# Three float32r passes of 12-bit parts in place of float32 matmuls with Strassen's form

## The chip, the cores and the metric

The kernel runs on one core of one Trainium2 chip. A core has TensorE (matmuls, whose results go to the memory PSUM), VectorE, ScalarE, GpSimd, and SyncE, which here only issues DMA transfers. The metric is the device time of one execution in microseconds, the median of several; the profile is one such execution. The kernel before took 689.4 us (three runs, 688.28 to 691.62).

## The reference

Two blocks follow each other: lightning attention over blocks of 64 tokens with a decaying state, and a two-layer block with a leaky ReLU.

```python
# q, k, v: (4, 8, 768, 64) float32; w_in (512, 2048), w_out (2048, 512) float64
for b in range(nb):                                   # blocks of 64 tokens
    intra = einsum('bhic,bhjc->bhij', qb, kb) * Dmask
    intra = einsum('bhij,bhjd->bhid', intra, vb)
    inter = einsum('bhid,bhde->bhie', qb * lam_pow, kv_state)
    out[:, :, sl] = intra + inter
    kv_state = lam_block * kv_state + einsum('bhsd,bhse->bhde', kb * rev_pow, vb)
x = out.transpose(0, 2, 1, 3).reshape(3072, 512)
h = x @ w_in                                          # "up"
return maximum(0.01 * h, h) @ w_out                   # "down", float32 (3072, 512)
```

The weights come as float64 and are made float32 on the chip, by integer operations on the two words of each number. The two large products, 3072 x 512 x 2048 each, are to have float32's precision, so one pass of a narrow type is not enough.

## The kernel before

It works on chunks of 128 tokens (24 of them) and groups of four chunks (six). Attention runs in float32 on TensorE: transposes of k and q, and 64x64 matmuls in the four quarters of the array ("quads").

```python
def quad(out, rows, lhsT, rhs, cols, start=False):
    nc.tensor.matmul(out[HALF[cols]], lhsT=lhsT[HALF[rows]], rhs=rhs[HALF[rows]], ...)
# a chunk: transpose k, transpose q (4 matmuls each), scores (16 quads), kv (16),
# own (16: scores times v), inter (16: state times q); then ONE copy into x:
run("ACT", 0.6, lambda: nc.scalar.copy(x, po.pop(b)[:, :, 0:HP, :]), ["inter"], ("x", b))
```

The large products are float32 matmuls in Strassen's form (Winograd's variant): seven half-size products in place of eight, with sums of quarters of x, of the weights and of the leaky ReLU's result g formed on VectorE and GpSimd. Up and down of a quarter of d_ff ("unit" u) follow each other, so g stays in SBUF. Two PSUM tags, Z and W, alternate.

```python
PROD = {"P1": ("A11", "B11"), "P2": ("A12", "B21"), "P3": ("S4", "B22"), "P4": ("A22", "T4"),
        "P5": ("S1", "T1"), "P6": ("S2", "T2"), "P7": ("S3", "T3")}
    ...
    def mult(tag, name, after, first=False):                  # one product, booked at us = 1.73
        if tag not in st:
            st[tag] = pp.tile([P, UP, T], F32, name=tag, tag=bank[tag])
        run("PE", us, lambda: mm(st[tag], name, first), after, tag)
    return [lambda: (mult("Z", "P1", ins("P1"), True), keep(0, "Z")),        # keep: copy by ScalarE
            lambda: (mult("W", "P2", ["tot1"] + ins("P2"), True), total(0, "W")),   # total: add by VectorE
            ...  # P6, P5, P7, P3, P4

# up: mm of one product                          (T = 256 columns, UP = 2)
for i in range(UP):
    for kk in range(2):
        nc.tensor.matmul(t[:, i, :], lhsT=w[:, kk, :], rhs=x[:, kk, :], ...)         # L571
# down: mm of one product                        (4 matmuls again)
        nc.tensor.matmul(t[:, m, :], lhsT=G[g, u][sa][:, i, m * P:(m + 1) * P],
                         rhs=WO[UP * u + i][:, SB[sb], :], ...)                      # L597
...
for n, (g, u, w) in enumerate((g, u, w) for g in range(NG) for u in range(NU) for w in range(2)):
    need((2 * u + w + 1) * NW // (2 * NU))                    # weights converted just ahead of use
    together((up, down)[w](g, u) if n else parts, ...)        # attention's parts in between
```

A half of a 256-wide pair of weights is loaded as float64 (512 KB) and made float32 by three ScalarE operations (the magnitude, and two that extract low bits) and VectorE operations (a shift and an integer add). A small scheduler in the kernel (`run`, with a duration booked for each step) decides the order in which instructions are issued; each engine then works in that order.

Of the kernel before, what the change touches and what calls it, by code (L numbers as in the profile page):

```python
# [8 lines left out]
F32 = mybir.dt.float32  # L37
I64 = mybir.dt.int64
I32 = mybir.dt.int32
# [6 lines left out]

def _bc(ap, idx, n):

    a = [list(x) for x in ap.ap]
    return bass.AP(ap.tensor, ap.offset, a[:idx] + [[0, n]] + a[idx:])  # L50


@with_exitstack
def kernel(
# [12 lines left out]
    B, H, S, D = q.shape  # L67
    C = P
    C2 = C // 2
    NCB = S // C  # L70
# [3 lines left out]
    FO = d_ff // P  # L74
# [3 lines left out]
    T = GC * C // 2  # L78
    NP = FO // 2
    HD = d_model // 2  # L80
    UP = 2
    NU = NP // UP
    NX = 3
    WARM = 10
    HALF = (slice(0, D), slice(D, 2 * D))
    assert D == 64 and KO == HP == 4 and S % C == 0 and NCH % GC == 0 and NP % UP == 0

    const = ctx.enter_context(tc.tile_pool(name="const", bufs=1))
    wop = ctx.enter_context(tc.tile_pool(name="wop", bufs=1))
    ldp = ctx.enter_context(tc.tile_pool(name="ldp", bufs=2))  # L90
    atp = ctx.enter_context(tc.tile_pool(name="atp", bufs=1))
    xp = ctx.enter_context(tc.tile_pool(name="xp", bufs=1))
    tp = ctx.enter_context(tc.tile_pool(name="tp", bufs=2))
    PS = bass.MemoryType.PSUM
    pp = ctx.enter_context(tc.tile_pool(name="pp", bufs=1, space=PS))

    ctx.enter_context(tc.manual_schedule(engines=None))


    lam_b = const.tile([P, H], F32, name="lam_b")  # L100
    nc.scalar.dma_start(out=lam_b, in_=lam.partition_broadcast(P))
    ident = const.tile([P, P], F32, name="ident")
    make_identity(nc, ident)

    idle = pp.tile([P, 2 * P], F32, name="idle", tag="W")
    for _ in range(WARM):
        nc.tensor.transpose(out=idle[:, 0:P], in_=ident, identity=ident)
    zero = const.tile([P, 1], F32, name="zero")
    nc.gpsimd.memset(zero, 0.0)

    lam_h = const.tile([P, H], F32, name="lam_h")
    lam_p = const.tile([P, HP], F32, name="lam_p")
    for i in range(2):
        nc.vector.tensor_copy(lam_h[:, i * HP:(i + 1) * HP], lam_b[:, i::2])
    for i in range(2):
        nc.vector.tensor_copy(lam_p[HALF[i]], lam_h[HALF[i], i::2])


    eye = atp.tile([P, C2], F32, name="eye", tag="sc")
    nc.vector.tensor_tensor(eye, ident[:, 0:C2], ident[:, C2:C], op=ALU.add)  # L120
    decay = const.tile([P, 2, HP, C2], F32, name="decay")
    for hi in range(2):
        for hp in range(HP):
            nc.vector.tensor_tensor_scan(decay[:, hi, hp, :], _bc(lam_h[:, 2 * hp + hi], 1, C2), eye, 0.0,
                                         op0=ALU.mult, op1=ALU.add)

    pow_q = const.tile([P, HP, C2], F32, name="pow_q")
    for hp in range(HP):
        nc.vector.tensor_tensor_scan(pow_q[:, hp, :], _bc(lam_p[:, hp], 1, C2), _bc(zero[:, 0], 1, C2), 1.0,
                                     op0=ALU.mult, op1=ALU.add)  # L130
    pow_k = decay[:, :, :, C2 - 1].rearrange("p hi hp -> p hp hi")
    lam_c = pow_q[:, :, C2 - 1]


    state = [const.tile([P, HP, D], F32, name=f"state{i}") for i in range(4)]

    QB = 2 * P
    SB = {"B21": 0, "B11": 1, "T4": 2, "B22": 3, "T1": 4, "T3": 5, "T2": 6, "B12": 2}  # L140
    WI, WO = [None] * NP, [None] * NP
    w_in_r = moe_w_in.rearrange("(ko ki) n -> ki ko n", ki=P)

    blocks = [(w, p, h) for u in range(NU) for w in ("wi", "wo") for p in range(UP * u, UP * u + UP) for h in range(2)]
    NW = len(blocks)

    ROOMS = ["st"] + [f"{w}{p}" for w, p, h in reversed(blocks) if h == 0 and p >= UP]


    LOADS = "cwcwcwwcwwwwwcwwcccwcwwcwwwwwwwwwwwwwwwwww" + "c" * NCH
    SLACK, AHEAD = (0.7, 0.3), (10.0, 14.0)

    T_DVE = [0, 4, 7, 9, 11, 15]

    FIRST, STEPS = 2, [2, 2, 1, 5, 5, 6, 3, 3, 0, 1, 0, 2, 0, 1, 0, 4]
    rooms = {}
    w_raw, lo, w_done = {}, {}, 0

    clk = {"PE": 0.0, "ACT": 2.0, "DVE": 8.0, "POOL": 1.0, "DMA": 0.5}

    ready, later = {}, {"ACT": [], "DVE": [], "DVE T": [], "POOL T": []}

    def run(eng, us, fn, after=(), gives=None, fill=True):
        t = max([ready.get(k, 0.0) for k in after], default=0.0)  # L170
        for e in (eng, eng + " T") if fill else ():
            while later.get(e) and emit(e, t + SLACK[alone]):
                pass
        clk[eng] = max(clk[eng], t) + us
        fn()
        if gives is not None:
            ready[gives] = clk[eng] + 0.1
        if eng != "DMA":
            pump()

    def emit(queue, until):

        can, us, fn, after, gives = later[queue][0]
        eng = queue.split()[0]
        if not can() or held and eng != queue or any(k not in ready for k in after):
            return False
# [50 lines left out]

# [458 lines left out]
```

## Time and profile before

| | |
|---|---|
| time | 689.4 us (688.28 to 691.62) |
| span of the profiled execution | 686.1 us |
| HBM read, written | 35.66 MB, 6.29 MB |
| a 128x512 float32 copy from PSUM on ScalarE | 585 to 592 ns |
| a 128x512 float32 sum with one PSUM operand on VectorE | 0.68 to 0.69 us |
| loads of 512 KB of weights, from issue to landing | 5.1 to 5.5 us |

In the profile, PE is the matmul side of TensorE and PEld its weight loads; DVE is VectorE, ACT ScalarE, POOL GpSimd, and SPq the queue of SyncE. A row of groups or of the timeline gives the source line, engine, operation, destination and sources by their names in the program, and the shape. The chain of waits is followed back from the last instruction, at each step to what released it. "PEclk" is the clock that TensorE was granted, in tenths of full speed, with 9 for 90% or more. The ends of matmuls are modelled, and their durations overlap, so the pace of matmuls is read from starts and not from durations.

### The profile page before, as it was taken

Reading aid. Unit: us, or ns where it says so; the run is one execution under the profiler, and the core shown is the slowest. Engines: PE = TensorE matmul, PEld = TensorE weight load, DVE = VectorE, ACT = ScalarE, POOL = GpSimd, SP = SyncE. Lnnn points to the kernel's source line nnn. Section 1 sums busy time; section 2 is a strip of 40 time slices with the busy share of each in tenths; the row PEclk is TensorE's granted clock in tenths of the full one; section 3 lists DMA queues with packets and bytes.
Section 4 is the critical chain, followed back from the end, with each engine's and each line's share of the span. In section 5 each row is a group of like instructions: output and inputs, shape, how many; then the busy total and the mean of one; then the engine's idle time right before and its main releaser. Section 6 shows DMA issues by size and latency. Waiting matters only on the chain.

```text
span 686.1 us, 13341 instructions
## 1 busy us (share of the span) xinstructions
PE 672.5 (98%) x5834; PEld 580.3 (85%) x5834; DVE 319.2 (47%) x474; ACT 213.2 (31%) x361; POOL 145.1 (21%) x141
## 2 busy tenths in 40 slices
PE   7799999999999999999999999999999999999997
PEld 6588888888888888888888888888888888888886
DVE  5897898572342552424425315244234245325324
ACT  5778866422222122230220321202122211221210
POOL 3565457551001033010113211204000003000000
PEclk9999999999999999999999999999999999999999
DMA  8996574513001004120210301000100000100001
GB/s 220 291 303 208 150 200 127 152 48 93 16 1 32 1 25 123 24 48 0 48 32 16 109 5 28 1 1 1 62 1 0 1 1 15 47 0 1 1 0 62
DMA packets 89050, 42.81 MB, mean 62 GB/s; under 512 B 76704, under 2 KB 82848, under 8 KB 88992
## 3 DMA queue, kind: packets, MB, share of 16 engines
q1 hardware_dynamic: 88848, 41.95, 22.0%
q8 instruction: 46, 0.75, 0.4%
q14 instruction: 12, 0.10, 0.0%
q10 hardware_dynamic: 144, 0.00, 0.0%
HBM read 35.66 MB, written 6.29 MB: 61 GB/s over the span
## 4 chain that ended last, share of the span: by engine, by line
PE 93%; DMA 3%; DVE 2%; SPq 1%; issue 1%; ACT 0%; POOL 0%; DVEq 0%
PE Z L571 24%; PE Z L597 23%; PE W L571 18%; PE W L597 18%; PE po L338 3%; PE pt L354 3%; DMA k<-in_k_dram 2%; PE ps L338 2%; PE pu L338 1%; DVE gS L542 1%; DVE gA L542 1%; DMA q<-in_q_dram 0%; SPq L327 0%; DVE os L521 0%; DVE wo L286 0%
## 5 line engine op out<-in xcount | busy, mean ns | idle before, releaser
L597 PE MATMUL Z<-wo,gA 128*128 128x256 f32 x576 | 137.5, 382 | 0.0
L597 PEld LDWEIGHTS Z<-wo,gA 128*128 128x128 f32 x576 | 107.8, 190 | 14.8
L571 PE MATMUL Z<-x,wi 128*128 128x256 f32 x384 | 92.2, 383 | 0.0
L571 PE MATMUL W<-xs,wi 128*128 128x256 f32 x384 | 92.0, 382 | 0.0
L597 PE MATMUL W<-wo,gA 128*128 128x256 f32 x384 | 91.0, 380 | 0.0
L571 PE MATMUL Z<-xs,wi 128*128 128x256 f32 x384 | 90.9, 380 | 0.0
L517 ACT COPY gA<-Z 128x512 f32<-128x512 f32 x48 | 28.1, 586 | 179.1 <-PE Z L571 178.8
L571 PEld LDWEIGHTS Z<-x,wi 128*128 128x128 f32 x384 | 72.7, 192 | 10.2 <-DVE wi L286 0.3
L571 PEld LDWEIGHTS Z<-xs,wi 128*128 128x128 f32 x384 | 72.8, 190 | 10.0
L597 PEld LDWEIGHTS W<-wo,gA 128*128 128x128 f32 x384 | 72.7, 190 | 10.0
L533 ACT ACTIVATE gA<-gA 128x512 f32<-128x512 f32 x72 | 45.3, 630 | 112.3 <-DVE gA L521 112.0
L571 PEld LDWEIGHTS W<-xs,wi 128*128 128x128 f32 x384 | 71.3, 190 | 9.6
L366 POOL TENSOR_TENSOR k<-k,decay 128x512 f32<-128x512 f32 (+1 forms) x24 | 27.6, 1150 | 219.7 <-PE pt L354 214.6
L521 DVE TENSOR_TENSOR gA<-gA,W 128x512 f32<-128x512 f32 x48 | 32.9, 686 | 87.3 <-PE W L571 87.3
L521 DVE TENSOR_TENSOR gA<-gA,Z 128x512 f32<-128x512 f32 x24 | 16.5, 687 | 97.8 <-PE Z L571 97.8
L420 POOL TENSOR_TENSOR state<-state,pow_q 128x256 f32<-128x256 f32 x40 | 28.1, 702 | 95.9 <-DVE state L417 89.2
L597 PE MATMUL W<-wo,gS 128*128 128x256 f32 x192 | 46.1, 383 | 0.5 <-DVE os L521 0.5
L597 PE MATMUL Z<-wo,gS 128*128 128x256 f32 x192 | 45.7, 381 | 0.5 <-DVE os L515 0.5
L571 PE MATMUL W<-x,wi 128*128 128x256 f32 x192 | 45.5, 380 | 0.0
L521 DVE TENSOR_TENSOR os<-os,W 128x512 f32<-128x512 f32 x48 | 32.8, 682 | 23.5 <-PE W L597 23.5
L597 PEld LDWEIGHTS W<-wo,gS 128*128 128x128 f32 x192 | 35.7, 189 | 6.9 <-DVE os L521 1.9
L597 PEld LDWEIGHTS Z<-wo,gS 128*128 128x128 f32 x192 | 36.0, 190 | 6.0 <-DVE os L515 0.9
(76 smaller groups left out, 721.9 us busy)
## 6 DMA issues: line engine op xcount, KB each, us to landing
ws<-in_moe_w_in_dram SPq DMA_DIRECT2D x16, 512.0 KB, 5.5
ws<-in_moe_w_out_dram SPq DMA_DIRECT2D x16, 512.0 KB, 5.1
k<-in_k_dram SPq DMA_DIRECT2D x48, 128.0 KB, 3.3
q<-in_q_dram SPq DMA_DIRECT2D x48, 128.0 KB, 2.9
v<-in_v_dram SPq DMA_DIRECT2D x24, 256.0 KB, 3.6
out_dram<-os SPq DMA_DIRECT2D x23, 256.0 KB, 2.1
out_dram<-os SPq DMA_DIRECT2D x2, 128.0 KB, 1.7
lam_b<-in_lam_dram ACTq DMA_DIRECT2D x1, 4.0 KB, 2.7
```

The source lines that it names most:

```text
L338: nc.tensor.matmul(out[HALF[cols]], lhsT=lhsT[HALF[rows]], rhs=rhs[HALF[rows]], start=start, stop=True, skip_group_check=True)
L354: nc.tensor.transpose(out=pt[:, y, :], in_=loaded[c][i][:, 2 * y:2 * y + 2, :].rearrange("p a d -> p (a d)"), identity=ident)
L366: run("POOL", 1.2, lambda: nc.gpsimd.tensor_tensor(kr[n], kr[n], _bc(pow_k, 3, D)[n], op=ALU.mult), [("pt", "k")], ("kd", c))
L420: run("POOL", 0.8, lambda: nc.gpsimd.tensor_tensor(state[(m + 1) % 4], new, _bc(lam_c, 2, D), op=ALU.mult), [("state", m)], ("lstate", m + 1))
L517: run("ACT", 0.6, lambda: nc.scalar.copy(dst(i), st[tag]), [tag], f"keep{i}")
L521: lambda: nc.vector.tensor_tensor(dst(i), dst(i), st[tag], op=ALU.add), [f"keep{i}", tag], f"tot{i}")
L533: run("ACT", 0.64, lambda: nc.scalar.activation(out=dst, in_=src, func=AF.Prelu, bias=0.0, scale=1.0, alpha=0.01), [after], gives)
L542: run(eng, us, lambda: e.tensor_tensor(t[o], t[a], t[b], op=op), after, ("sum", eng, o))
L571: nc.tensor.matmul(t[:, i, :], lhsT=w[:, kk, :], rhs=x[:, kk, :], start=(first and i == 0 and kk == 0), stop=(i == UP - 1 and kk == 1), sk ...
L597: nc.tensor.matmul(t[:, m, :], lhsT=G[g, u][sa][:, i, m * P:(m + 1) * P], rhs=WO[UP * u + i][:, SB[sb], :], start=(first and m == 0 and i ...
```

## The change

Each operand is split into parts that float32r, TensorE's reduced float32, holds exactly: a high part h of 12 bits and the rest l. In Karatsuba's manner three products suffice for a float32 result in place of the hardware's four passes: h times h', l times l', and (l - h) times (h' - l') with suitable powers of two. The first two are summed in one PSUM bank (b1), the third in another (b2), and the result is b1 * (1 + 1/4096) + b2. Strassen's form is given up, and with it all its sums of quarters.

The three parts of one weight matrix take 3 x 8 x 4 KB = 96 KB of each SBUF partition (eight pairs p of 256 of the 2048 columns), so only one of the two weight matrices can be there at a time. The kernel therefore has two phases: first attention and "up" for all six groups, with g written to memory; then, with w_out's parts in place of w_in's, "down" for all groups, with g read back and split there. w_out is made float32 during the first phase and goes through memory as well.

```diff
-    ...                      # the old scheduler, Strassen's products and sums
+class Plan:                  # steps are added with engine, booked us, reads, writes and rank, and then
+    ...                      # ordered: the step that can begin first goes first, by rank among equals
+    W = [[sb([P, 4 * 2 * P], f"w{x}{p}", F32R) for x in "hlm"] for p in range(NP)]
+    X = [[sb([P, KO, T], f"x{x}{i}", F32R) for x in "hlm"] for i in range(2)]      # two groups
+    b1, b2 = ps([P, T], "b1"), ps([P, T], "b2")
+    G = [[dram.tile([P, 2 * T], F32, ...) for p in range(NP)] for g in range(NG)]
 # a chunk of attention: the same matmuls; its result is split in parts
-        run("ACT", 0.6, lambda: nc.scalar.copy(x, po.pop(b)[:, :, 0:HP, :]), ["inter"], ("x", b))
+        add("ACT", 0.6, ... activation(out=tok(xs[i]), in_=y, func=AF.Copy, scale=S) ...)
+        add("ACT", 0.6, ... activation(out=tok(xh), in_=y, func=AF.Copy, scale=NEAR) ...)
+        add("DVE", 0.75, ... scalar_tensor_tensor(xl, xh.bitcast(F32), -S, xs[i], ...) ...)
+        add(("DVE", "POOL"), (0.75, 1.2), lambda e: ENG[e].tensor_tensor(xm, xh..., xl..., op=ALU.subtract), ...)
 # weights: the same conversion to float32, and then
+    def parts(p, src, keys):
+        add(("ACT", "DVE"), (1.05, 0.7), head, keys, [f"wh{p}"])
+        add(("DVE", "POOL"), (1.3, 2.3), ... wl = src - wh ...)
+        add("DVE", 1.3, ... wm = wl - wh / S ...)
 # up, for group g and pair p
+        def product(dst, f, z, start):
+            for kk in range(KO):
+                nc.tensor.matmul(dst, lhsT=w[z][:, kk * 2 * P + f * P:kk * 2 * P + (f + 1) * P], rhs=x[z][:, kk, :], ...)
+        for f in range(2):
+            add("PE", 0.91, lambda f=f: product(b1, f, 0, True), keys("h"), ["b1"])
+            add("PE", 0.91, lambda f=f: product(b1, f, 1, False), keys("l"), ["b1"])
+            add("ACT", 0.6, ... activation(out=t, in_=b1, func=AF.Copy, scale=1.0 + 1.0 / S) ..., rank=-1.5)
+            add("PE", 0.91, lambda f=f: product(b2, f, 2, True), keys("m"), ["b2"])
+            add("DVE", 0.69, ... tensor_tensor(r, t, b2, op=ALU.add) ..., rank=-1.5)
+        add("ACT", 1.05, ... activation(out=y, in_=y, func=AF.Prelu, scale=S, alpha=0.01) ...)
+        add("DMA", 1.5, ... nc.sync.dma_start(out=G[g][p], in_=y...) ...)
 # down: load, split, multiply
+    def down_load(g, p):
+        add("DMA", 1.5, ... nc.sync.dma_start(out=graw[j], in_=G[g][p]) ...)
+        add("ACT", 1.05, ... h ...); add("DVE", 1.3, ... l ...); add(("DVE", "POOL"), (1.3, 2.3), ... m ...)
+    def down(g, p):
+        for tb in range(GC):                                  # four accumulators at once, in eight PSUM tiles of 512 columns
+            for pp in (p, p + 1):
+                def go(tb=tb, pp=pp, j=j):
+                    for f in range(2):
+                        for z in range(3):
+                            nc.tensor.matmul(acc[tb][z // 2], lhsT=ring[j][z][:, f * T + tb * P:...],
+                                             rhs=W[pp][z][:, f * d_model:(f + 1) * d_model], ...)
+                add("PE", 1.36, go, ...)
 # order of the up steps; a chunk of attention after each while it may, then w_out's conversions
-    for n, (g, u, w) in enumerate((g, u, w) for g in range(NG) for u in range(NU) for w in range(2)):
+    steps = [(0, p) for p in range(4)] + [(1, p) for p in range(4)] + [(g, p) for g in range(2) for p in range(4, NP)]
+    steps += [(g, p) for g in range(2, NG) for p in range(NP)]
```

Here T is 512: a group's four chunks are one matmul of 512 columns. A group's x parts are held for two groups at a time, so a chunk of group g can be written only when the up steps of group g - 2 are done. `po` and `psc`, the PSUM tiles of attention, are single; k, q, v and their transposes are double.

## The prediction

> **What bounds the kernel now.** I read the page in this order: the span and the busy shares, the chain that ended last, the groups of matmuls, and then a timeline of the late kernel, where nothing but the two large products is left.
>
> ```profile
> span 686.1 us, 13341 instructions
> PE 672.5 (98%) x5834; PEld 580.3 (85%) x5834; DVE 319.2 (47%) x474; ACT 213.2 (31%) x361; POOL 145.1 (21%) x141
> PEclk9999999999999999999999999999999999999999
> ...
> PE 93%; DMA 3%; DVE 2%; SPq 1%; issue 1%; ACT 0%; POOL 0%; DVEq 0%
> PE Z L571 24%; PE Z L597 23%; PE W L571 18%; PE W L597 18%; PE po L338 3%; PE pt L354 3%; DMA k<-in_k_dram 2%; PE ps L338 2%; PE pu L338 1%; DVE gS L542 1%; DVE gA L542 1%; DMA q<-in_q_dram 0%; SPq L327 0%; DVE os L521 0%; DVE wo L286 0%
> ```
>
> TensorE is the bound: 93% of the chain, 98% busy, at full granted clock. L571 and L597, the up and the down product, are 83% of the chain; L338 and L354, the attention, are 9% (the finer view has 3.2 + 3.0 + 1.9 + 1.4 = 9.5%, or 65 us, 2.7 us for each of the 24 chunks of 128 tokens). So only TensorE time matters, as long as the other engines keep up; VectorE is at 47%.
>
> A busy TensorE need not be one at its pace, so I take the pace from the starts of successive products in the timeline (start, duration, engine, what):
>
> ```profile
> 640.71 1.89 PE L571 MATMUL Z<-xs,wi 128*128 128x256 f32 x8
> 642.44 1.89 PE L571 MATMUL W<-xs,wi 128*128 128x256 f32 x8
> 644.17 1.89 PE L571 MATMUL Z<-x,wi 128*128 128x256 f32 x8
> 645.89 1.89 PE L597 MATMUL Z<-wo,gA 128*128 128x256 f32 x8
> ```
>
> From 640.71 to 645.89 are three products: 1.727 us each. One product is four matmul calls, and the trace has eight records for it, so a float32 matmul leaves two records of 1.727/8 = 215.9 ns. The kernel has 6 groups x 4 units x 2 x 7 = 336 products: 336 x 1.727 = 580 us. With the attention that is 580 + 65 = 645; the rest of the span, 41 us, is the start, waits and the end.
>
> The start matters because the change rearranges it. These rows of the timeline show the first chunks:
>
> ```profile
> 3.89 1.12 PE L354 MATMUL pt<-ident,k 128*128 128x128 f32 x4
> ...
> 10.44 0.94 PE L354 MATMUL pt<-ident,k 128*128 128x128 f32 x4
> ...
> 15.06 0.66 PE L354 MATMUL pt<-ident,k 128*128 128x128 f32 x4
> ...
> 21.16 1.12 PE L354 MATMUL pt<-ident,k 128*128 128x128 f32 x4 [0.70 <-DMA k<-in_k_dram]
> ...
> 23.02 2.73 PE L571 MATMUL Z<-x,wi 128*128 128x256 f32 x8
> ```
>
> A chunk takes 5.8 us at the start (3.89 to 21.16 for three) though it has only some 2.8 us of matmuls; the large products begin at 23 us, on half a group. The same view by stretches gives what else is loaded then (busy us of each engine, clock, DMA share, GB/s):
>
> ```profile
> 0.00:20.00 20.00, 14.93 (x367) 12.20 (x371) 12.08 (x31) 10.39 (x17) 7.41 (x15) 1.00 0.91 236
> 20.00:40.00 20.00, 16.68 (x266) 12.87 (x261) 17.17 (x24) 15.81 (x28) 11.86 (x11) 0.91 0.97 295
> 40.00:60.00 20.00, 20.00 (x238) 17.02 (x231) 18.39 (x25) 15.55 (x27) 11.52 (x12) 1.00 0.98 279
> ```
>
> The DMA engines are at 91 to 98% for 60 us, at 236 to 295 GB/s, and VectorE and ScalarE at 80 to 90% from 20 us on. This is the one stage where something other than TensorE is near its limit.
>
> **What the Trainium skill says.** "TensorE: Matmul & The Clock Gate", section "Wait — 56ns, not 53.3ns?", puts back-to-back matmuls at columns / 2.4 GHz + 2.5 ns, 215.7 ns for 512 columns. "Perfetto Trace Analysis", section "Engine Utilization", halves the array's rate for the float32 low/high mode. The trace agrees with both at once: a record of 256 columns takes 215.9 ns, so it is two passes, and a float32 matmul is four. The same page, section "Optimizing Tensor Performance", wants matmul groups to rotate through PSUM banks so that one is emptied while the next fills; the change leaves one bank for each kind of sum, see below. "SBUF — State Buffer", section "Who interferes with whom", says that a VectorE operation with two SBUF inputs contends with GpSimd. The trace agrees: gS<-gA,gA took 1.46 us at 143.25 us, with GpSimd at work, and 0.69 us at 646.72 us, without.
>
> **The change part by part.**
>
> (a) Large products. Removed: 1344 float32 matmuls of 256 columns, 580 us. Added: up 6 x 8 steps x 2 halves x 3 passes x 4 = 1152 matmuls of 512 columns, down 6 x 8 x 4 x 2 x 3 = 1152; 2304 in all. If a float32r matmul is one pass, it has 512 columns like a record of before, 215.9 ns: 497 us. The column count alone says the same: Strassen has 7/8 x 4 = 3.5 passes, the new form 3. But the source books 0.91 us for four of them, 227.5 ns, where the kernel before booked 1.73 us for a product that the trace shows at 1.727: its author's figures look measured. That would be 524 us. No record of a float32r matmul is at hand, so I take the middle, 221.7 ns: 511 us, a saving of 69. Their weight loads should hide: 190 ns per 128x128 float32 load in the groups, under 216.
>
> (b) Attention on TensorE: the same transposes and 64x64 quads, 24 x 2.8 = 67 us, unhidden as before (2.8 rather than 2.7, as the chain drops what overlaps).
>
> (c) The start. The new up product wants all four chunks of a group, where before three were enough, and the whole of a chunk's parts (two ScalarE copies at about 0.59 us, two VectorE operations of about 0.7 us) lies behind it. If the fourth chunk begins where it did, at 21.2 us, and takes the 6.5 us that the first took on TensorE (3.89 to 10.44) and then 2 x 0.59 + 2 x 0.7 = 2.6 us for its parts, the first up product comes at 30 us. The instruction order has the scores and sums of a fifth chunk ahead of the first up product, so TensorE has about 13 us of work in these 30: 17 us idle.
>
> (d) The first four steps, each with a chunk and a w_in pair to convert. TensorE: 24 x 0.2217 + 2.8 = 8.1 us. ScalarE, from the durations of before: conversion 2 x (0.67 + 0.79 + 0.77) = 4.5, chunk 4 x 0.59 = 2.4, step 2 x 0.59 + about 1.05 = 2.2; 9.1. VectorE: conversion 2 x (0.42 + 0.95) = 2.7, parts of the weights 0.7 + 1.3 + 1.3 or 2.0 with one of them on GpSimd, chunk 0.69 + 0.84 + 0.15 + 0.75 = 2.4, step 2 x 0.69 = 1.4; 8.5 to 9.8, before contention. DMA: 0.79 + 1.05 + 0.52 MB = 2.4 MB at 280 GB/s, 8.4 us. All sit at 8.5 to 10 us, so a step is about 10 us: 4 x 2 = 8 us idle. In the next twelve steps almost no chunk is new, and the remaining conversions catch up.
>
> (e) From there TensorE sets the pace, with b1 and b2 as the only two accumulators. b1 must be emptied by ScalarE (0.59 us, about 0.05 us of wait on each side in the timeline) while the third pass, 4 x 0.22 = 0.89 us, runs: 0.2 us of slack, lost when ScalarE is in a Prelu of 1024 columns (about 1.05 us) or a chunk's copy. I put 8 us on all 96 of these. Once, at group 2, whose chunks can only start when group 0 is done, about 3 us.
>
> (f) Down product: g comes back through memory, 512 KB each, in place 4 to 5 us after issue. A pair of tiles is 48 matmuls, 10.6 us; behind it lie ScalarE 2.1, VectorE and GpSimd 5.2 us. It stays hidden. The turn from up to down is 3 us, the end (copy 0.6, sum 0.69, store 2) about 4.
>
> (g) VectorE loses Strassen's sums, off the path already: no gain of time.
>
> Sum: 511 + 67 + 17 + 8 + 8 + 3 + 3 + 4 = 621 us of span. The time is 3.3 us above the span before (689.4 against 686.1): **624 us**.
>
> **The rivals.** First, float32r runs at two passes, or its weight load does not hide: 216 + 190 ns a matmul would make over 900 us. For it: no such record is in the profile. Against it: the change counts three passes in place of four, and books 227 ns. Small. Second, the evacuation of b1 becomes the bound: if each of 96 halves waited 0.5 us, plus 40 us. For it: one bank, in-order ScalarE with Prelu, attention copies and conversions in the same queue. Against it: ScalarE would be at 2.2 of 5.3 us in a step without a chunk, and attention matmuls can fill in. It would give 655 to 660. Third, the traffic: 25 MB of g each way and 4 MB of w_out each way, so about 101 MB instead of 42.8. Over 620 us that is some 165 GB/s, against 295 shown at the start; only if loads stood in the SyncE queue behind stores that wait would TensorE see it, some 10 to 30 us. Fourth, the best case: matmuls at 215.9 ns and 30 us of idle, 497 + 67 + 30 + 3 = 597.
>
> **Range and chances.** The low end is the fourth rival, 597. The high end is matmuls at 227.5 ns and 60 us of idle: 524 + 67 + 60 + 3 = 654, so 655. For slower than 2%, the first rival or a plan that stalls in general has to hold; for a result within 2%, all of the saving has to be eaten. Faster 0.90, same 0.04, slower 0.06.
>
> **What would show it right or wrong.** The starts of successive up products: four matmuls in 0.86 to 0.91 us; 1.7 or more kills (a). The first up product near 30 us, (c). The granted clock at full after it. The waits of TensorE: below about 10 us for b1 and b2 together, (e); if ScalarE or VectorE are its first releasers with 30 us or more, the second rival holds. Waits for the tiles that come from memory near nothing, (f). TensorE busy 92 to 95%. I am wrong if the matmul pace falls outside 212 to 230 ns, or if TensorE's idle time outside the first 70 us exceeds 35 us.

## The result, and the profile after

The changed kernel takes 664.1 us (median of four runs, 662.0 to 666.7), the kernel before 690.3 us in the same comparison: ratio 0.963, 95% interval 0.960 to 0.966. It is faster by 26 us; I had forecast a gain of 65, and 664 lies above the range of 597 to 655. The profile is of the slowest of the four runs, 666.65 us.

The page of the changed kernel (the span; busy time, share and instructions of each engine; the granted TensorE clock in 40 slices; the chain that ended last, by engine and by line):

```profile
span 662.8 us, 13107 instructions
PE 637.4 (96%) x5450; PEld 505.2 (76%) x5450; DVE 359.9 (54%) x481; ACT 285.8 (43%) x412; POOL 93.2 (14%) x96
PEclk8887999999999999999999999999999999999999
...
PE 85%; DMA 4%; DVE 3%; ACT 3%; issue 2%; SPq 1%; POOL 0%; ACTq 0%; DVEq 0%; POOLq 0%
PE b L432 37%; PE po L482 10%; PE psc L482 10%; PE pt L482 10%; PE b L482 10%; PE po L225 3%; PE pt L260 2%; DMA raw<-in_moe_w_in_dram 2%; PE psc L225 2%; DMA wo<-w 1%; PE pt L225 1%; SPq L251 1%; DMA att<-in_v_dram 1%; DVE w L385 1%; DVE xm L349 1%
```

TensorE is still the bound, and at 96% looks busier than I forecast (92 to 95%). But its share of the chain has fallen from 93 to 85%, with DMA, VectorE and ScalarE in it at 3 to 4% each, and the clock is not full in the first slices, where I had expected it full once the products begin. L432 is the up product, L482 the down product.

The pace is read as before, from the starts. In the down product of the changed kernel (timeline: start, duration, engine, what):

```profile
402.72 0.39 PE L482 MATMUL po<-wh,xh 128*128 128x512 f32 x1
402.95 0.39 PE L482 MATMUL po<-wl,xl 128*128 128x512 f32 x1
...
405.44 0.39 PE L482 MATMUL b<-wh,xh 128*128 128x512 f32 x1
```

Twelve matmuls from 402.72 to 405.44 are 226.7 ns each: one record a matmul, so one pass, but 11 ns longer than a record of before. The durations of 0.39 overlap and say nothing of the pace.

**Where the 662.8 us are.** From the starts in the trace I counted three things by stretch: large matmuls at 226.7 ns; attention at its own pace inside a block (32.6 ns a quad, 109 ns a transpose record); and the "loss", which is what remains of the stretch. Within the loss, a *turn* is what TensorE needs more than that pace where it goes from products to a block of attention and back: the last product matmul before attention (on average over all turns in the middle of the kernel about 305 ns), the last record of attention (about 110, where 38 is usual), and the first product matmul after it (about 330).

| | predicted | in the trace |
|---|---|---|
| (a) 2304 matmuls | 511 | 522.3 |
| (b) attention, 24 chunks | 67 | 69.9 |
| turns, 84 of them | none | 21.4 |
| (c) loss before the first up product | 17 | 20.7 |
| (d) the first steps, up to 100 us, turns apart | 8 | 14.5 |
| (e) the rest of the up phase, turns apart | 11 | 9.1 |
| (f) turn to down, and end | 7 | 4.8 |
| sum | 621 | 662.7 |

The kernel before has 63 turns, 14.8 us, counted in the same way. So the 42 us that I missed are half turns (21), a quarter pace (11), a quarter the start (10), and 3 of attention, less 4 that I had put too high in (e) and (f).

The averages hide two kinds of turn. 68 of the 84 blocks of attention hold quads; where a block has quads alone, the three steps at its edges take 319, 149 and 338 ns, together 0.31 us too much. The other 16 blocks hold transposes alone, whose tile is 128x128 like that of the products. From the last product before such a block to the second after it, the median loss is 0.01 us. The kernel before has the same two kinds, 43 blocks with quads at 0.31 us and 19 of transposes at less than 0.01. So the 21.4 us, which count every turn with the same three steps, are about 1 us too high.

**The start.** The first up product in the timeline of the changed kernel:

```profile
35.30 1.19 PE L432 MATMUL b<-xh,wh 128*128 128x512 f32 x4 [0.32 <-ACT xh L345]
```

It comes at 35.3 us, not 30. And a stretch of the first steps shows VectorE held up:

```profile
50.23 1.15 POOL L269 TENSOR_TENSOR att<-att 64x512 f32<-64x512 f32 x1 [6.60 <-PE pt L260]
...
50.50 5.01 DVE L349 TENSOR_TENSOR xm<-xh,xl 128x512 fp32r<-128x512 f32 x1
...
51.34 2.37 POOL L396 TENSOR_TENSOR wl<-w,wh 128x1024 fp32r<-128x1024 f32 x1
...
53.68 1.27 POOL L275 TENSOR_TENSOR att<-att 128x512 f32<-128x512 f32 x1
...
56.16 1.38 PE L432 MATMUL b<-xm,wm 128*128 128x512 f32 x3 [3.12 <-DVE gs L446]
```

The difference xm<-xh,xl is booked at 0.75 us in the source. It runs 5.01 us, from 50.50 to 55.51, beside three GpSimd operations that follow each other without a gap, from 50.23 to 54.95. TensorE then waits 3.12 us; the wait is put down to gs, the sum that stood behind xm in VectorE's queue.

A third part is the clock. From 39.4 to 42.8 us and from 56.5 to 63.3 us TensorE is granted half of it, and a product matmul takes some 427 ns in place of 226.7:

```profile
60.81 1.91 PE L432 MATMUL b<-xl,wl 128*128 128x512 f32 x4
62.65 1.21 PE L225 MATMUL po<-att 64*64 64x64 f32 x48
```

From 60.81 to 62.65 are four matmuls. Fifteen such matmuls add up to 3.1 us, a part of the 14.5 in (d) for this profiled run. No run isolates why the clock fell there.

**The bank b1.** A late stretch of the changed kernel, where only up products are left:

```profile
347.11 1.08 PE L432 MATMUL b<-xm,wm 128*128 128x512 f32 x4
...
347.37 0.60 ACT L443 ACTIVATE t<-b 128x512 f32<-128x512 f32 x1 [0.19 <-PE b L432]
348.02 0.76 PEld L432 LDWEIGHTS b<-xh,wh 128*128 128x128 f32 x4 [0.25 <-ACT t L443]
348.03 1.19 PE L432 MATMUL b<-xh,wh 128*128 128x512 f32 x4
```

The m pass (into b2) starts at 347.11, but ScalarE can read b1 only at 347.37, 0.26 us later; its copy ends at 347.97, and the next weight load waits 0.25 us for it. The first h matmul then takes 332 ns instead of 227, since its weight load is not covered. The wait stands on the weight load's row (PEld), which the list of groups confirms for the whole kernel:

```profile
L432 PE MATMUL b<-xh,wh 128*128 128x512 f32 x384 | 114.4, 420 | 4.0 <-ACT xh L345 2.5 <-ACT t L443 1.4
...
L432 PEld LDWEIGHTS b<-xh,wh 128*128 128x128 f32 x384 | 65.6, 190 | 23.7 <-ACT t L443 8.9 <-ACT xh L345 3.1
```

The last column is idle time before the group and its main releasers: the weight loads stand 8.9 us behind b1's copy t, the matmuls themselves only 1.4.

### The profile page after: what moved, and what is told of

It is laid out like the page before. It is cut to its first block, busy times and chain, and to the rows that moved or that the text cites. A ratio compares the mean times of both kernels' runs of the same rounds, so it can differ in the third digit from the quotient of the medians.

```text
span 662.8 us, 13107 instructions
## 1 busy us (share of the span) xinstructions
PE 637.4 (96%) x5450; PEld 505.2 (76%) x5450; DVE 359.9 (54%) x481; ACT 285.8 (43%) x412; POOL 93.2 (14%) x96
## 4 chain that ended last, share of the span: by engine, by line
PE 85%; DMA 4%; DVE 3%; ACT 3%; issue 2%; SPq 1%; POOL 0%; ACTq 0%; DVEq 0%; POOLq 0%
PE b L432 37%; PE po L482 10%; PE psc L482 10%; PE pt L482 10%; PE b L482 10%; PE po L225 3%; PE pt L260 2%; DMA raw<-in_moe_w_in_dram 2%; PE psc L225 2%; DMA wo<-w 1%; PE pt L225 1%; SPq L251 1%; DMA att<-in_v_dram 1%; DVE w L385 1%; DVE xm L349 1%
## 5 line engine op out<-in xcount | busy, mean ns | idle before, releaser
L446 DVE TENSOR_TENSOR gs<-t,b 128x512 f32<-128x512 f32 x96 | 65.8, 686 | 105.3 <-PE b L432 80.5
L432 PE MATMUL b<-xh,wh 128*128 128x512 f32 x384 | 114.4, 420 | 4.0 <-ACT xh L345 2.5
L432 PE MATMUL b<-xm,wm 128*128 128x512 f32 x384 | 105.7, 398 | 4.7 <-DVE gs L446 3.1
L468 DVE SCALAR_TENSOR_TENSOR xl<-xh,att 128x1024 fp32r<-128x1024 f32 x48 | 58.6, 1221 | 93.7 <-ACT xh L467 93.7
L432 PE MATMUL b<-xl,wl 128*128 128x512 f32 x384 | 106.1, 398 | 0.9 <-DVE xl L347 0.9
L443 ACT ACTIVATE t<-b 128x512 f32<-128x512 f32 x96 | 57.2, 596 | 96.9 <-PE b L432 96.5
L432 PEld LDWEIGHTS b<-xm,wm 128*128 128x128 f32 x384 | 72.1, 190 | 21.2 <-DVE gs L446 3.5
L432 PEld LDWEIGHTS b<-xl,wl 128*128 128x128 f32 x384 | 71.6, 189 | 18.3 <-DVE xl L347 1.8
L432 PEld LDWEIGHTS b<-xh,wh 128*128 128x128 f32 x384 | 65.6, 190 | 23.7 <-ACT t L443 8.9
L470 DVE TENSOR_TENSOR xm<-xh,xl 128x1024 fp32r<-128x1024 f32 x48 | 58.8, 1225 | 4.8
L482 PE MATMUL psc<-wm,xm 128*128 128x512 f32 x96 | 37.3, 389 | 0.0
L482 PE MATMUL po<-wh,xh 128*128 128x512 f32 x96 | 37.3, 389 | 0.0
L482 PE MATMUL pt<-wh,xh 128*128 128x512 f32 x96 | 37.3, 389 | 0.0
L482 PE MATMUL psc<-wl,xl 128*128 128x512 f32 x96 | 37.3, 389 | 0.0
L482 PE MATMUL b<-wl,xl 128*128 128x512 f32 x96 | 37.3, 389 | 0.0
L482 PE MATMUL b<-wm,xm 128*128 128x512 f32 x96 | 37.3, 389 | 0.0
```

The source lines that it names most:

```text
L432: nc.tensor.matmul(dst, lhsT=w[z][:, kk * 2 * P + f * P:kk * 2 * P + (f + 1) * P], rhs=x[z][:, kk, :], start=start and kk == 0, stop=kk == ...
L443: add("ACT", 0.6, lambda t=t: nc.scalar.activation(out=t, in_=b1, func=AF.Copy, bias=0.0, scale=1.0 + 1.0 / S), ["b1"], [f"t{jt}"], rank=-1.5)
L446: add("DVE", 0.69, lambda t=t, r=r: nc.vector.tensor_tensor(r, t, b2, op=ALU.add), [f"t{jt}", "b2"], [f"gs{jg}"], rank=-1.5)
L468: add("DVE", 1.3, lambda: nc.vector.scalar_tensor_tensor(l, h.bitcast(F32), -S, graw[j], op0=ALU.mult, op1=ALU.add), reads + [f"rh{j}"], w ...
L470: add(("DVE", "POOL"), (1.3, 2.3), lambda e: ENG[e].tensor_tensor(m, h.bitcast(F32), l.bitcast(F32), op=ALU.subtract), [f"rh{j}", f"rl{j}" ...
L482: nc.tensor.matmul(acc[tb][z // 2], lhsT=ring[j][z][:, f * T + tb * P:f * T + (tb + 1) * P], rhs=W[pp][z][:, f * d_model:(f + 1) * d_model ...
```

## The experiments

A loss below is always the one defined above. "On e3" means that the edit is made to the kernel of e3, 658.6 us.

### e1: what a matmul costs by form

In the down product, group 1 is done in pieces of 256 columns, group 4 in pieces of 128, group 2 with bfloat16 (the high halves of the words, so with less precision), group 3 with plain float32 matmuls; groups 0 and 5 stay.

```diff
+if g == 2:   lhs, rhs = lhs.bitcast(BF16)[:, 1::2], rhs.bitcast(BF16)[:, 1::2]
+elif g == 3: lhs, rhs = lhs.bitcast(F32), rhs.bitcast(F32)
+n = {1: 2, 4: 4}.get(g, 1)          # pieces of 512 / n columns
```

> In the down phase, where TensorE waits for nothing, each group of 192 products of 512 columns takes another form: group 0 and 5 as they are (226.7 ns a matmul in the changed kernel), 1 as two float32r matmuls of 256 columns, 2 as bfloat16 (the high halves of the same words; it leaves precision out), 3 as plain float32, 4 as four float32r matmuls of 128 columns. Theory A, a fixed cost of some 13 ns for each float32r matmul over its columns: about 120 ns a matmul in group 1, 67 in group 4, and about 216 in group 2 if the cost is float32r's alone. Theory B, the weight load of float32 words sets a floor under each matmul: group 1 and 4 stay near 190 to 227 ns a matmul, so that they take almost two and four times as long as group 0, and bfloat16 goes to 216. Theory C, the clock or the memory: all groups are 6% above their columns, bfloat16 at 227 too. Plain float32: two records of 430 to 440 ns.

A single run, 831.4 us. The timeline of e1, in the order 256 columns, bfloat16, float32, 128 columns:

```profile
455.18 0.40 PE L493 MATMUL b<-wm,xm 128*128 128x256 f32 x2
...
457.10 0.40 PE L493 MATMUL pt<-wl,xl 128*128 128x256 f32 x2
```

```profile
520.23 0.39 PE L493 MATMUL b<-wh,xh 128*128 128x512 bf16 x1
...
522.03 0.39 PE L493 MATMUL b<-wm,xm 128*128 128x512 bf16 x1
```

```profile
600.55 1.02 PE L493 MATMUL psc<-wh,xh 128*128 128x512 f32 x2
601.41 1.02 PE L493 MATMUL psc<-wl,xl 128*128 128x512 f32 x2
```

```profile
699.80 0.61 PE L493 MATMUL b<-wh,xh 128*128 128x128 f32 x4
700.25 0.61 PE L493 MATMUL b<-wl,xl 128*128 128x128 f32 x4
```

Starts divided by records: 256 columns (457.10 - 455.18)/16 = 120 ns; bfloat16 at 512 columns 1.80/8 = 225; float32 at 512 columns 0.86/2 = 430 a record; 128 columns 0.45/4 = 112. Going from 256 to 512 columns takes a matmul from 120 to 226.7 ns, so 106.7 ns are columns (256 at 2.4 a ns) and 13 ns come with the one-pass matmul at both widths; bfloat16 at 512 has nearly the same 12. A float32 record carries only about 2.5 (215.9 = 213.3 + 2.6 at 256 columns, 430 = 426.7 + 3 at 512). At 128 columns something else sets a floor of 112, where a fixed cost of 13 ns alone would give 67. "TensorE: Matmul & The Clock Gate", section "Wait — 56ns, not 53.3ns?", of the Trainium skill (columns / 2.4 GHz + 2.5 ns) so agrees with the float32 records and not with float32r and bfloat16 here, where each matmul has new weights; the measurement decides. My expectation of 216 for bfloat16 failed: the extra is not float32r's own. Why float32 escapes it stays open.

### e2: a shorter copy out of b1

ScalarE copies only 256 of the 512 columns of b1, and the sum uses these twice; half of the correction sums is left out.

```diff
-nc.scalar.activation(out=t, in_=b1, func=AF.Copy, ...)
+nc.scalar.activation(out=t[:, 0:T // 2], in_=b1[:, 0:T // 2], func=AF.Copy, ...)
```

> ScalarE copies only the first 256 columns of b1 (the sum reads them twice; half of the result is left out), in about 0.33 us in place of 0.60, in the same order of instructions. If the single bank b1 costs TensorE a bare weight load at each turn (about 106 ns on the first matmul of an h pass that follows an m pass directly), those first matmuls fall from about 332 to about 230 ns, the stretch without attention before the down phase goes from 239.6 to about 229 ns a matmul, and the time falls by 3 to 6 us. If the 0.1 us is a cost of going back to b1 whatever ScalarE does, nothing changes.

659.8 us, ratio 0.954 (0.952 to 0.955): 4.3 us less. The timeline of e2 in the late stretch:

```profile
342.45 1.08 PE L432 MATMUL b<-xh,wh 128*128 128x512 f32 x4
...
345.19 1.08 PE L432 MATMUL b<-xh,wh 128*128 128x512 f32 x4
```

A half step is 345.19 - 342.45 = 2.74 us; in the changed kernel the h pass alone lasts 0.1 us longer. The first h matmul after m falls from 332 to 233 ns, and the loss from 340 to 388 us from 3.3 to about 1 us. So the copy's length was the wait.

### e3: GpSimd taken off the parts

xm of the activations and wl of the weights run on VectorE alone; before, the plan could give them to GpSimd.

```diff
-add(("DVE", "POOL"), (0.75, 1.2), lambda e: ENG[e].tensor_tensor(xm, ...
+add("DVE", 0.75, lambda: nc.vector.tensor_tensor(xm, ...
-add(("DVE", "POOL"), (1.3, 2.3), lambda e: ENG[e].tensor_tensor(wl, ...
+add("DVE", 1.3, lambda: nc.vector.tensor_tensor(wl, ...
```

> The low and middle parts of x and of the weights are formed on VectorE alone, never on GpSimd, in the first phase. If VectorE's two-input operations were held up by GpSimd's (a 128x512 difference of 5.0 us at 50.5 us and of 2.7 us at 36.8 us), these two go back to 0.7 to 1.5 us, TensorE's loss in the first 100 us falls from 39 us by 5 to 8 us and the time by 4 to 8 us. If VectorE is just full of conversions then, its extra 1.2 us a step makes the time the same or up to 5 us longer.

658.6 us, ratio 0.952 (0.951 to 0.954), though VectorE got more work. The same group in the list of groups, first of the changed kernel, then of e3 (count | busy us, mean ns | idle):

```profile
L349 DVE TENSOR_TENSOR xm<-xh,xl 128x512 fp32r<-128x512 f32 x21 | 23.6, 1125 | 0.7
```

```profile
L349 DVE TENSOR_TENSOR xm<-xh,xl 128x512 fp32r<-128x512 f32 x24 | 20.1, 836 | 0.7
```

VectorE does 24 of them in less time than 21 before. The loss up to 100 us falls from 39.5 to 32.3 us, most of it between 35 and 60 us (from over 10 to 4.2). The contention of VectorE with GpSimd is what the Trainium skill says in "SBUF — State Buffer", section "Who interferes with whom", and the 5.01 us above agree. Taking GpSimd off the parts is worth 5.5 us of time, a size that I had not put in. How much of it is contention alone is not separated: the five operations that moved were also longer on GpSimd (three xm of 1.29 us, two wl of 2.56), and the profile of e3 has no half clock in the first 100 us, which makes up about 3 us of the difference in loss.

### e4 and e11: no conversion of w_in

One ScalarE operation per half takes the place of the conversion from float64; the integer work is left out, so the weights are not the reference's. e4 does so in the changed kernel, e11 on e3.

```diff
+if kind == "wi":
+    add("ACT", 0.67, lambda: nc.scalar.activation(out=dst, in_=words(1, F32), func=AF.Abs, scale=1.0), ...)
+    return
```

> The conversion of w_in from float64 is left out but for one ScalarE operation per half (the loads stay, the values are wrong). If conversions on VectorE and ScalarE are what holds up the first 100 us, TensorE's loss there falls from 39 us to about 25 us and the time by 12 to 16 us, most of it between 35 and 100 us. If attention's own chain and the loads set the start, the first up product stays at 33 to 36 us and the time falls by less than 6 us.

e4: 659.4 us, ratio 0.953 (0.951 to 0.956). The first up product still comes at 35.3 us, and the loss up to 100 us is 34.3 us: 5 less.

> Both suspects of the start are taken out at once: w_in's conversion is left out but for one operation of ScalarE per half (wrong values), and the parts are formed on VectorE alone. If VectorE's list of work sets the first 100 us, TensorE's loss there falls from 32 us (parts on VectorE) or 34 us (no conversion) to about 25 us, and the time to about 652 us. If the chain from chunk to chunk sets it, the loss stays above 30 us and the time at 656 to 659.

e11: 657.0 us, ratio 0.953 (0.950 to 0.956); first up product at 33.3 us, loss 30.2 us. That is hardly better than e3. So neither w_in's conversion nor GpSimd's share in the parts explains the bulk of the loss at the start: without both TensorE still loses 30 us in the first 100. Contention itself is not gone in e11: attention's own steps keep GpSimd busy for 39 of these 100 us, and one xm<-xh,xl still takes 2.68 us (at 44.97 us). In the trace the first chunks follow each other through DMA, ScalarE, GpSimd, VectorE and back to TensorE, each step with its own latency. The longest pieces of the changed kernel's chain before its first product are two loads, 5.68 us for v (from 8.22 us) and 5.29 us for a half of w_in (from 16.94 us). That this chain is the cause is argued from the trace only, and no run takes the loads away.

### e5: b1 emptied by two engines

On e3, from the ninth step: ScalarE takes one half of b1's columns, VectorE the other.

```diff
+add("ACT", 0.33, ... nc.scalar.activation(out=t[:, 0:T // 2], in_=b1[:, 0:T // 2], func=AF.Copy, ...)
+add("DVE", 0.33, ... nc.vector.tensor_scalar(t[:, T // 2:T], b1[:, T // 2:T], 1.0 + 1.0 / S, None, op0=ALU.mult)
```

> On the kernel with all parts formed on VectorE. From the ninth up step on, b1 is emptied by ScalarE and VectorE at once, 256 columns each, so the whole result is kept. If the bare weight load comes from b1 being free 0.1 us too late, this gives what the half copy gave: first matmuls of h after m from 332 to about 230 ns, and the time falls by 3 to 5 us from that kernel's 658.6. If VectorE, which works in order and has attention and conversions too, comes later than ScalarE did, nothing is gained or up to 3 us are lost.

670.7 us, ratio 0.971 (0.968 to 0.975): worse by 12 us than e3. The timeline of e5 says why:

```profile
344.07 0.38 ACT L444 ACTIVATE t<-b 128x256 f32<-128x256 f32 x1 [2.26 <-PE b L432]
344.49 0.42 DVE L446 TENSOR_SCALAR t<-b 128x256 f32<-128x256 f32 x1 [1.93 <-ACT t L444]
344.97 0.76 PEld L432 LDWEIGHTS b<-xh,wh 128*128 128x128 f32 x4 [0.51 <-DVE t L446]
```

The halves do not run together: here VectorE waits for ScalarE, and 0.38 + 0.42 us plus a handover take longer than the single copy of 0.60. In all 80 pairs of the trace one follows the other (ScalarE is first in 56, and in these VectorE's half carries a wait for a semaphore of ScalarE). So this is an order that the program was given, and the run does not show what would happen without it. The weight load now waits 0.51 us instead of 0.25, and over the whole kernel weight loads stand 21.2 us behind the two operations, where e3 has 8.8 behind the one. That the wait grew and the time with it agrees with e2 from the other side. It need not be all of the 12 us: the loss from 340 to 388 us grew from 2.9 to 7.6 us, but the new steps also changed the plan's order, and the first product comes at 37.4 us in place of 34.4.

### e6 and e8: two other orders for the start

On e3, e6 lets the conversions of w_in come later in the plan's order; e8 books longer DMA times in the plan.

```diff
-plan.rank = n - 4.0        # e6
+plan.rank = n - 2.5
-add("DMA", 1.6, load, ...) # e8
+add("DMA", 2.4, load, ...)
```

> On the kernel with all parts formed on VectorE. The first weights are ranked behind the second chunk, so the second chunk's k, q and v are loaded ahead of them. If the start is held up by loads that stand behind 1 MB of weights (v of the second chunk landed 5.7 us after its issue), the second chunk's transposes come 2 to 4 us earlier than 10.95 us and the first up product 2 to 4 us earlier than 34.4 us, with the time down by as much. If the chain from chunk to chunk (state, decay, copies on engines that work in order) sets the start, the first up product moves by less than 1 us.

e6: 659.8 us, ratio 0.955 (0.952 to 0.958). The second chunk's transposes come 1.5 us earlier (9.27 instead of 10.78), the first up product later (35.1 instead of 34.4). No gain.

> On the kernel with all parts formed on VectorE. The plan books loads as long as they were (1.3 us for k, q or v, 2.4 for 512 KB of float64, 2.6 to land, in place of 1.15, 1.6 and 2.0), so that VectorE and ScalarE, which work in the planned order, do not stand before work whose data is late. If that is a part of the loss at the start (decay of the second chunk was done 2.8 us after its scores), TensorE's loss in the first 100 us falls from 32 us by 3 to 6 us. If not, the time is within 2 us of 658.6.

e8: 663.4 us, ratio 0.960 (0.957 to 0.963). The first up product comes at 33.0 us, but from 60 to 100 us nearly 14 us are lost (2.5 of them at half clock). What the plan moves at the start it gives back later.

### e7: fewer turns

On e5, the plan adds 0.15 us wherever TensorE goes between attention and products, so it keeps to one kind longer. The trace has 26 turns there and back, where e5 has 69 (the expectation counts each way, 53 and 139).

```diff
+turn = e == "PE" and self.kinds[i] != kind
+late = turn * 0.15          # added to the start that the plan compares
```

> On the kernel with b1 emptied by two engines. The plan is told that TensorE loses 0.15 us at each turn between attention and the products, and so makes about 53 turns in place of 139. If a turn costs what the trace shows (338 against 227 ns for the first product after attention, some 318 for the last one ahead, 150 for the last quad: 0.3 us for there and back), the first matmuls and last quads together lose about 13 us less. But attention is then done late and in one piece ahead of each group, where TensorE waits for its chain: I expect that to cost more than it saves, so that the time rises by 5 to 20 us, with the waits concentrated before groups 2 to 5.

700.5 us, ratio 1.014 (1.010 to 1.018): 30 us slower than e5, and 1.4% slower than the kernel before. The timeline of e7 where a block of attention stands alone (the last bracket is idle time and its releaser):

```profile
276.07 0.69 PE L233 MATMUL psc<-att 64*64 64x64 f32 x32
...
277.62 0.93 PE L233 MATMUL po<-att 64*64 64x64 f32 x48 [0.39 <-DVE att L292]
278.48 0.66 PE L268 MATMUL pt<-att 128*128 128x128 f32 x4
```

Without products in between, TensorE waits for VectorE and the others inside the chunk. The stretches 260 to 300 and 340 to 380 us lose 14.0 and 18.2 us, where e5 loses 4.3 and 5.8. The turns themselves, counted as above, fell from about 18 to 7 us. Interleaving costs turns, but hides more than it costs. e5's wait is in this kernel too, so its time alone does not price a turn; e12 does.

### e9 and e10: a third bank for the products

On e3, the attention's small results move into unused halves of another bank, q is transposed in pt0, and the bank pt1 serves the up product: h and l alternate between b1 and pt1. e10 adds e6's order.

```diff
+b3 = pt[1].rearrange("p y t -> p (y t)")
-add("PE", 0.91, lambda f=f: product(b1, f, 0, True), keys("h"), ["b1"])
+add("PE", 0.91, lambda f=f, bb=bb: product(bb, f, 0, True), keys("h"), [kb])   # b1 or b3
```

> On the kernel with all parts formed on VectorE. The sums of k and v are written to the unused halves of the score banks and q is transposed in the bank of k, which frees one PSUM bank after the fourth chunk: the two halves of an up step then alternate between two banks for h and l. If the single bank b1 is what costs a bare weight load at each turn, the first matmuls of h after m fall from 332 to about 230 ns, the stretch without attention goes from 239 to about 229 ns a matmul, and the time falls by 3 to 6 us from 658.6. If attention's tighter banks cost more than that, the time is the same or rises.

e9: 659.1 us, ratio 0.955 (0.953 to 0.958), as e3. From 340 us on the loss is gone (about 0 instead of 3.0 in the attention-free stretch), but the start is worse: first up product at 37.4 us, 38.7 us lost up to 100.

> The same with the first weights ranked behind the second chunk, so that its loads and its VectorE work come first: if the order at the start matters in this form, 1 to 3 us less than with three banks alone; if, as before, the start is set by the work on VectorE, within 2 us of it.

e10: 653.4 us, ratio 0.947 (0.944 to 0.950), the best of all: it beats the changed kernel by 10.8 us. Its first up product is at 35.1 us, the loss up to 100 us 30.3. The timeline of e10:

```profile
342.34 1.07 PE L433 MATMUL b<-xm,wm 128*128 128x512 f32 x4
...
344.15 1.07 PE L433 MATMUL pt<-xh,wh 128*128 128x512 f32 x4
345.06 1.07 PE L433 MATMUL b<-xm,wm 128*128 128x512 f32 x4
```

345.06 - 342.34 = 2.72 us for twelve matmuls: every h pass at the full pace of 226.7, after a bank change as after none. This is the rotation of banks that the prediction quotes. Its worth depends on the order at the start: with e6's order the third bank gains 6.5 us (659.8 to 653.4), 3 of them in the stretch without attention and about as much in the first 100 us (loss 33.0 to 30.3); with e3's order it gains nothing. Why the start goes better with it in the one order and worse in the other is not shown.

### e12: what a turn costs

On e3, the last up group (no attention is left then) gets extra matmuls in the middle of each pass of four: one 64x64 float32 quad in steps three and four, one full 128x128 float32r matmul of 64 columns in steps five and six, nine quads in the last two. They compute nothing that is wanted, so only the passes' times are read.

```diff
 nc.tensor.matmul(dst, lhsT=w[z][...], rhs=x[z][:, kk, :], ...)
+if g == NG - 1 and kk == 1 and p in (4, 5):
+    nc.tensor.matmul(psc[:, 0, 0, :], lhsT=w[z][:, 0:P], rhs=x[z][:, 0, 0:C2], ...)
+elif g == NG - 1 and kk == 1 and p > 1:
+    for i in range(1 if p < 4 else 9):
+        quad(psc[:, i % 2, i // 2 % 2, :], i % 2, w[z][:, 0:C2].bitcast(F32), ...)
```

> Theory: going from 128x128 matmuls to 64x64 quads and back costs TensorE about 0.31 us (seen as longer steps at the seams: 338 and 318 ns beside a product, 149 beside a quad, where 227 and 38 are usual), a cost my prediction did not have. In the attention-free last up group, extra matmuls are put in the middle of every pass of four: one 64x64 quad in the third and fourth step, one full 128x128 matmul of 64 columns in the fifth and sixth, nine quads in the last two. A pass takes about 0.93 us without. Theory: with one quad 0.31 + 0.04 more, 1.28 us; with the full matmul only the floor of some 0.11 us more, 1.04; with nine quads 0.31 + 9 x 0.038 more, 1.58. Rival (the seams are waits of the attention, a semaphore or a bank, not the change of tile): one quad adds no more than 0.1 us, 1.0, and the full matmul about as much. Rival 2 (any foreign matmul in a pass costs the same, by its new bank): quad and full matmul both add about 0.3.

A single run, 675.5 us. The timeline of e12: a pass without anything (353.89), then with one quad (359.49), one full matmul (375.76), nine quads (388.79):

```profile
353.89 1.07 PE L432 MATMUL b<-xl,wl 128*128 128x512 f32 x4
354.80 1.07 PE L432 MATMUL b<-xm,wm 128*128 128x512 f32 x4
...
359.49 0.73 PE L432 MATMUL b<-xh,wh 128*128 128x512 f32 x2
...
360.62 0.33 PE L225 MATMUL psc<-xl,wl 64*64 64x64 f32 x2
360.87 0.73 PE L432 MATMUL b<-xl,wl 128*128 128x512 f32 x2
...
375.76 0.71 PE L432 MATMUL b<-xh,wh 128*128 128x512 f32 x2
...
376.80 0.71 PE L432 MATMUL b<-xl,wl 128*128 128x512 f32 x2
...
388.79 0.73 PE L432 MATMUL b<-xh,wh 128*128 128x512 f32 x2
...
390.40 0.73 PE L432 MATMUL b<-xl,wl 128*128 128x512 f32 x2
```

From a start to the same place in the next pass: 0.91 us plain, 1.38 with one quad, 1.04 with the full matmul, 1.61 with nine quads. A full matmul costs 0.13 us, as its 112 ns floor in e1 says. A single quad, four times smaller, costs 0.47; eight more quads add only 0.23. No attention is in between, and the full matmul goes to the same bank psc, so both rivals fall. The matmul before the quad takes 327 ns and the one after it 335 to 345, as beside attention. I had expected 1.28 for the single quad: its own two records are longer alone (107 and 148 ns) than in a row.

The quad differs from the full matmul in its type too: float32 against float32r. The traces of the two kernels settle that. In the kernel before, products, quads and transposes are all float32, and its blocks with quads lose 0.31 us, its blocks of transposes less than 0.01. And in the changed kernel transposes, which are float32 but 128x128, stand between float32r products at almost no cost. First a block of 8 quads (two records each), then one of four transposes:

```profile
104.25 1.07 PE L432 MATMUL b<-xm,wm 128*128 128x512 f32 x4
105.25 0.46 PE L225 MATMUL po<-att 64*64 64x64 f32 x16
...
106.67 1.08 PE L432 MATMUL b<-xl,wl 128*128 128x512 f32 x4
...
110.39 1.08 PE L432 MATMUL b<-xm,wm 128*128 128x512 f32 x4
111.31 0.60 PE L260 MATMUL pt<-att 128*128 128x128 f32 x4
...
112.69 1.08 PE L432 MATMUL b<-xl,wl 128*128 128x512 f32 x4
```

From 104.25 to 106.67 are two passes and the quads, 2.42 us, of which 8 x 0.2267 + 8 x 0.0326 = 2.07 are work: 0.35 us too much. From 110.39 to 112.69 are two passes and the transposes, 2.30 us, of which 8 x 0.2267 + 4 x 0.109 = 2.25 are work: 0.05. So it is the change of tile size that costs, and not the type, the bank or the attention.

## Why the prediction was wrong, step by step

The mechanism was right: three passes for three and a half, one pass per float32r matmul, TensorE the bound after the start, the traffic hidden. The sum was too small by 42 us, in four of its terms and in one that it did not have.

- **The missing term, turns: 21 us.** Step (b) took attention at 24 x 2.8 us and priced the rest of the up phase only by bank waits. I had set the 41 us left over in the kernel before down as "the start, waits and the end"; some 15 of them were turns, and I carried none over. The change made 84 of 63 (68 of 43 with quads, the ones that cost); all the attention now stands in the first 340 us, where before it went on to 499. e12 shows the cost of such a turn, and the two traces its number; e7 shows that they can't simply be saved. Attention at its own pace was 69.9 us instead of 67.
- **(a), the pace: +11.** 226.7 ns instead of 221.7. The two candidates were 215.9 and the 227.5 that the source books, and I took the middle; the booked one was right, e1. The argument that a float32r matmul costs what a float32 record of equal columns costs fell: the extra of some 13 ns came with the one-pass matmuls of both types.
- **(c) and (d), the start: +10.** (c): 35.3 us instead of 30, loss 20.7 instead of 17. (d): 14.5 instead of 8. The words "before contention" in (d) were part of the fault: taking GpSimd off the parts is worth 5.5 us (e3), and w_in's conversion up to 5 (e4), though the two together hardly more (e11). Another 3 us were half clock, where I had expected it full. What holds the rest, about 30 us of loss in the first 100 in e11, was not isolated: the cause of this term stays open.
- **(e), the banks: the sum right, its working wrong.** 9 us instead of 11. I gave b1 "0.2 us of slack". The copy can start only 0.26 us after the m pass does, and the weight load of 0.19 us must follow it: 0.26 + 0.60 + 0.05 + 0.19 = 1.10 us against a pass of 0.91. Of the 0.19 us that this would cost, the starts show about 0.1 in every half step without attention inside (e2, e9), not only in those beside a Prelu. Attention in between covers it in the others, which keeps the sum small.
- **(f) held.** No loss at the turn to down (0.2 us from 388 to 402), 4.6 at the end. The third rival, traffic, is out: 101.5 MB were moved as forecast, and TensorE never waits for g.
- **The rivals.** The first is out (one pass, loads covered). The second, b1's evacuation as the bound, named the right bank and far too large a size. Its 96 x 0.5 us, or 40 more than (e), would have given 624 + 40 = 664 us and not the 655 to 660 written there; that the time came out at 664 is chance. My signs were partly blunt, and neither of the two that I had named as showing me wrong (a pace outside 212 to 230 ns, over 35 us idle outside the first 70) came true: the matmuls' waits for b1 and b2 stayed below 10 us and busy time rose to 96%, because a turn is booked as busy time and b1's wait stands at the weight load. Only the starts show both.

## What to carry to other kernels

A remainder that a profile of before leaves unexplained has to be taken apart before the forecast, for the change carries it over and may multiply it: here a third of "start, waits and end" were seams between tile sizes, and a busy share hid them. Price a new matmul form by its own starts, or by the figure that a tuned source books, not by another type's record. And for a bank with one owner, count the whole loop: drain, copy, handover and the bare weight load, against the work that covers it.

## What the runs showed of the hardware

- One-pass matmuls with new weights each carry about 13 ns beside their columns (float32r 226.7 ns at 512 columns, 120 at 256; bfloat16 225 at 512), float32 records only about 2.5 (215.9 at 256, 430 at 512); at 128 columns float32r takes 112 ns.
- Between 128x128 matmuls, one 64x64 float32 quad costs 0.47 us, a full matmul of 64 columns 0.13 (e12). A block of quads between products loses 0.31 us at its edges, one of 128x128 transposes 0.01 or less, in both kernels and with products of either type.
- A VectorE difference of 128x512, 0.69 us at its best, took 5.0 us beside GpSimd operations that followed each other closely.
- In two stretches of the changed kernel's first 100 us TensorE was granted half its clock while products ran, and a float32r matmul of 512 columns took 427 ns there.
